# One order table of a fused attention and gated convolution kernel is exchanged for another

## The chip, the core and the metric

The kernel runs on one core of a Trainium2 chip. The metric is the device time in microseconds (us) of one execution; the kernel before took 237.97 us, the median of three runs (237.76 to 238.59). Five engines work side by side, each through its own list of instructions in order: PE (TensorE, matrix products), DVE (VectorE), ACT (ScalarE), POOL (GpSimd) and SP (SyncE, which issues all the DMAs here). An instruction that waits holds up everything behind it on its engine, and nothing on the others until they need it.

## The reference

For 4 batches, 8 heads, 768 positions and a head width of 64, each query sees its neighbours nearer than 16 positions and 24 block summaries (the maximum of the keys and the mean of the values of each block of 32). The 512 wide result then goes through a causal convolution of 5 taps per channel, whose sigmoid gates a linear map, and through a second linear map.

```python
mask_l = np.abs(pos[:, None] - pos[None, :]) < window
scores_s = scale * np.einsum('bhsd,bhnd->bhsn', q, k_sum) + np.log(block)
a = softmax(concatenate([where(mask_l, scores_l, -1e9), scores_s]))
x = a @ concatenate([v, v_sum])             # then heads side by side: B, S, 512
gate = 1 / (1 + exp(-sum_k conv_w[k] * x[s - 4 + k]))
out = (gate * (x @ w_val)) @ w_out
```

## The kernel before

A group g (0 to 11) is 256 positions of one batch; a unit u (0 to 23) is half a group's heads, so that group g holds the units 2g and 2g+1. Most pieces of work come in two halves (.0 and .1) of a unit or of a group.

Nothing in the kernel schedules itself. The string `ORDER` is a list of 955 words; line 729 goes through it, and each word calls one function, which adds its instructions to the lists of its engines. The position of a word against the others of its engine is the order in which that engine works. Tiles come from pools with few buffers (line 54 and the pools of lines 131 to 145); a write into a buffer waits until the earlier tile in it has been read.

```python
for word in ORDER.split():
    nm_ = word.rstrip("0123456789.")
    ops[nm_](*(int(a) for a in word[len(nm_) :].split(".") if a))
```

The words, by engine:

- PE: `W` warm-up products on zeros; `s` scores (L528); `t` transposes of the weights (L579); `x` values (L596, and L598 for group 0); `v` the linear map with w_val (L653, eight passes for group 0, which runs in full float32, twelve for the others); `o` the map with w_out (L690; group 0 has eight small pieces `o0.0.0` to `o0.1.3`, whose last number is the block of 128 columns of w_out); `vb` and `vsp` transposes of block summaries.
- DVE: `n` mask and row extreme (L544); `r` reciprocals of the row sums (L564, L565); `T` the four taps of the convolution (L633); `gf` gate times value (L659); `ks` block maxima of the keys (L225); `sh` and `or`, the two steps that put a block of 64 bit weights together as float32, a shift (L363) and a join (L367); `tv1.3`, one summary of values (L249).
- ACT: `e` exponentials (L557); `c` copies of transposed weights (L586); `X` and `Y` copies of the attention result (L607, L611); `I` the first tap (L627); `G` the gate (L640); `gh` and `ob` copies (L664, L700); `rb` (L358) and `wc` (L403) for the weights.
- POOL: `m` normalising (L569); `Z` and `gl` rests of the split into two parts (L615, L667); `tv` a tree of five additions that sums the values of a block (L253); `kc`, `wl`, `hal` small ones.
- SP: loads `L...` (`Lu` the transposed values for `tv`, `Lv` the values, `Lwo` w_out), `F` which writes block summaries into the value tile (L332), `O` the stores.

A copy `c` frees the one PSUM tile that the transposes `t` of the next half are written to. The value tiles of `Lu` (L209) have two buffers, so a third load waits for a tree on POOL (or, for `tv1.3`, on DVE). The assembled weights `wf` have one buffer of four blocks: w_val's blocks are used up before w_out's are joined into them.

Of the kernel before, what the change touches and what calls it, by code (L numbers as in the profile page):

```python
# [61 lines left out]
vc3.0 vc2.1 vc3.1 vc2.0 s4.1 vb1 n4.0 rbwv2 c1.1 vbc1 n4.1 x1.0 rbwv0 e3.1 rbwv3 wlwv1 m2.1 m2.0
shwv0 shwv2 s5.0 t2.0 x1.1 orwv0 shwv3 orwv2 orwv3 s5.1 Lk1.0 Lk1.1 n5.0 r3 c2.0 Y1 T0.1 n5.1
e4.0 wcwv3 e4.1 v0.1.0 t2.1 v0.0.0 G0 m3.1 wcwv2 Lk1.2 c2.1 wlwv3 m3.0 I1 r4 Lu1.2 v0.1.1 m4.0
F1 Lq3 t3.0 e5.0 m4.1 c3.0 v0.0.1 t3.1 x2.0 e5.1 ks1.1 x2.1 ks1.0 T1.0 c3.1 Lk1.3 wlwv2 X2 Y2
# [2 lines left out]
v1.1.0 n7.1 wlwv0 e6.1 c4.0 rbwo1 v1.1.1 F2 m5.1 m5.0 tv1.1 v1.0.0 t5.0 Lu1.0 Lwo2 v1.0.1 x4.0
e7.0 rbwo0 shwo0 orwo0 shwo1 x4.1 s8.0 orwo1 c5.0 G2 X4 rbwo2 shwo2 s8.1 orwo2 t5.1 Lwo3 Y4 c5.1
wcwo0 gf1.0 r6 rbwo3 e7.1 wcwo2 Lu1.3 o0.0.0 o0.0.1 tv1.3 Lv3 o0.0.2 shwo3 x5.0 orwo3 tv1.0 x5.1  # L70
vsp1 vsc1 m6.0 t6.0 Lq5 o0.0.3 o0.1.0 Lu2.0 Lk3.0 Lu2.2 F3 o0.1.1 o0.1.2 o0.1.3 r7 n8.0 n8.1
s9.0 I3 ob0.0 X5 s9.1 wcwo3 Y5 c6.0 T3.0 T3.1 Z4 m6.1 wlwo0 t6.1 n9.0 e8.0 wcwo1 n9.1 hal2 m7.1
Z5 m7.0 v2.0.0 x6.0 c6.1 G3 I4 gh1.0 x6.1 s10.0 s10.1 gf1.1 t7.1 wlwo2 wlwo1 Lk2.2 Lk2.1 gl1.0
gh1.1 e8.1 X6 T4.0 v2.0.1 v2.1.0 T4.1 ob0.1 O0.0 c7.1 tv2.0 wlwo3 gl1.1 hal3 tv2.2 Y6 G4 t7.0
n10.0 r8 gf2.0 I5 c7.0 e9.0 e9.1 gh2.0 v2.1.1 T5.0 T5.1 Lu2.3 n10.1 o1.0 o1.1 m8.1 t8.1 ob1.0
Lv4 G5 r9 ks2.2 Lk2.0 gf2.1 s11.0 s11.1 I6 T6.0 c8.1 gh2.1 m8.0 gl2.0 e10.0 gl2.1 m9.0 kc2.2
x7.0 x7.1 t8.0 T6.1 n11.0 ks2.1 ks2.0 Lq6 c8.0 ob1.1 X7 Y7 o2.0 Lk2.3 m9.1 Lv5 o2.1 G6 e10.1
ob2.0 F4 I7 Z7 r10 n11.1 Z6 m10.1 kc2.1 kc2.0 T7.0 e11.0 t9.0 v3.1.0 x8.0 x8.1 c9.0 s12.0 T7.1
e11.1 s12.1 t9.1 X8 n12.0 Lu2.1 v3.1.1 n12.1 r11 ks2.3 tv2.3 hal4 m10.0 c9.1 G7 Y8 t10.1 I8
v3.0.0 x9.0 Lq7 O1.0 x9.1 e12.0 c10.1 T8.0 gf3.1 X9 kc2.3 Y9 O1.1 T8.1 s13.0 s13.1 t10.0 c10.0  # L80
e12.1 Z8 m11.0 Z9 ob2.1 F5 tv2.1 v3.0.1 v4.0.0 t11.0 G8 v4.1.0 I9 x10.0 n13.1 n13.0 r12 x10.1
m12.1 s14.0 s14.1 e13.0 c11.0 gf3.0 vsp2 T9.0 T9.1 gh3.0 m11.1 gh3.1 t11.1 X10 vsc2 c11.1 Lk3.3
Y10 Lq8 G9 Lk3.1 v4.1.1 gl3.0 gl3.1 m12.0 I10 n14.1 gf4.1 n14.0 hal5 Z10 o3.0 e13.1 t12.0 c12.0
x11.0 x11.1 s15.0 O2.1 Lv6 s15.1 t12.1 T10.0 v4.0.1 e14.0 e14.1 r13 T10.1 n15.0 m13.1 gf4.0
n15.1 o3.1 Lu3.2 X11 F6 Lv7 G10 O0.1 F7 Y11 Lu3.0 c12.1 r14 I11 m13.0 Z11 m14.1 t13.1 s16.0
T11.0 T11.1 gh4.0 c13.1 ob3.1 ob3.0 e15.0 m14.0 s16.1 x12.0 x12.1 ks3.0 n16.1 t14.1 c14.1 tv3.2
hal6 v5.0.0 t13.0 v5.1.0 v5.1.1 n16.0 ks3.1 Y12 kc3.1 G11 gl4.0 c13.0 X12 I12 x13.0 x13.1 Lq9
s17.0 s17.1 O3.1 Lk3.2 T12.0 gh4.1 e16.0 e15.1 Y13 t14.0 Z12 v5.0.1 T12.1 gf5.1 c14.0 r15 e16.1
ks3.2 kc3.0 n17.0 gf5.0 gl4.1 tv3.0 G12 m15.0 hal7 I13 e17.0 X13 n17.1 o4.1 O3.0 o4.0 s18.0
s18.1 x14.0 x14.1 t15.0 ks3.3 kc3.3 m15.1 Z13 ob4.1 e17.1 X14 v6.1.0 c15.0 T13.0 r16 ob4.0 Y14  # L90
t15.1 T13.1 G13 gh5.0 I14 v6.0.0 v6.1.1 x15.0 O4.1 Lu3.3 O4.0 c15.1 r17 n18.0 n18.1 kc3.2 m16.1
x15.1 gl5.0 T14.0 s19.0 T14.1 e18.0 gh5.1 Y15 e18.1 s19.1 t16.1 v6.0.1 tv3.3 gl5.1 Z14 gf6.1
n19.0 m17.0 m16.0 m17.1 o5.1 gf6.0 o5.0 G14 O2.0 I15 X15 r18 n19.1 c16.1 gh6.1 t16.0 ob5.1 gh6.0
Lv8 Lq10 T15.0 s20.0 Lu3.1 F8 T15.1 s20.1 c16.0 x16.0 m18.0 hal8 Z15 gl6.1 e19.0 x16.1 t18.0 Y16
c18.0 G15 v7.0.0 t17.0 tv3.1 v7.0.1 Lv9 Lq11 I16 c17.0 e19.1 n20.1 t17.1 v7.1.0 gf7.0 n20.0 r19
c17.1 gl6.0 m18.1 m19.1 X16 vsp3 t18.1 x17.0 x17.1 s21.0 c18.1 vsc3 T16.0 s21.1 T16.1 e20.0
t19.1 n21.0 e20.1 v7.1.1 n21.1 gf7.1 r20 m19.0 o6.0 o6.1 s22.0 X17 e21.0 Y17 G16 F9 I17 s22.1
gh7.0 c19.1 gh7.1 ob6.1 T17.0 e21.1 m20.0 T17.1 hal9 Z16 x18.0 x18.1 t19.0 Z17 v8.1.0 O5.1 Lv10
gl7.1 r21 gl7.0 ob5.0 n22.1 o7.0 X18 c19.0 ob6.0 G17 Y18 I18 t20.0 F10 v8.0.0 T18.0 n22.0 x19.0
x19.1 s23.0 c20.0 ob7.0 e22.0 s23.1 m20.1 t20.1 v8.1.1 e22.1 T18.1 Y19 G18 c20.1 I19 X19 m21.0  # L100
O6.0 Lv11 n23.1 n23.0 r22 o7.1 m22.1 Z19 T19.0 gf8.1 t21.0 v8.0.1 c21.0 x20.0 gf8.0 x20.1 O7.0
F11 O6.1 m21.1 Z18 t22.1 v9.1.0 c22.1 gh8.0 Y20 T19.1 gh8.1 G19 I20 X20 m22.0 v9.1.1 t21.1 c21.1
v9.0.0 x21.0 x21.1 hal10 e23.0 t22.0 gl8.0 gf9.1 T20.0 v9.0.1 T20.1 e23.1 r23 Y21 gf9.0 c22.0
G20 X21 ob7.1 gh9.1 gl8.1 I21 T21.0 gh9.0 o8.0 o8.1 m23.1 Z21 hal11 m23.0 gl9.0 ob8.1 gl9.1 o9.1
Z20 t23.1 v10.1.0 x22.0 x22.1 T21.1 O5.0 G21 c23.1 ob9.1 t23.0 X22 I22 Y22 c23.0 v10.0.0 v10.1.1
T22.0 gf10.1 x23.0 x23.1 v10.0.1 gf10.0 T22.1 gh10.1 X23 Y23 ob8.0 gh10.0 O8.1 O7.1 o9.0 ob9.0
gl10.1 Z22 G22 gl10.0 o10.1 Z23 I23 v11.0.0 T23.0 T23.1 v11.0.1 v11.1.0 gf11.0 v11.1.1 ob10.1
gh11.0 O8.0 G23 o10.0 gf11.1 gh11.1 O9.0 O9.1 gl11.0 gl11.1 o11.0.1 o11.1 ob10.0 ob11.0.1 O10.1
ob11.1 O10.0 O11.0.1 O11.1 o11.0.0 ob11.0.0 O11.0.0
# [694 lines left out]
```

## Time and profile before

| what | us |
|---|---|
| median of 3 runs | 237.97 |
| the profiled execution | 237.77 |
| its span, first to last instruction | 236.1 |
| PE busy in it | 224.9 (95%) |
| ACT busy | 190.6 (81%) |
| DVE busy | 184.2 (78%) |
| POOL busy | 152.2 (64%) |

The 1.7 us between the profiled execution's time and its span lie before the first and behind the last instruction. Busy times of the engines overlap; matrix products are pipelined, so the end of a row of PE can lie up to 0.2 us behind the start of the next. In the rows below a bracket at a row's end tells how long the engine was idle before it, and what ended that.

### The profile page before, as it was taken

How to read it: one execution, taken by the hardware profiler on the slowest of the kernel's cores; microseconds unless marked ns; L12 is line 12 of the kernel's file. 1: busy time of each engine (PE TensorE's matmuls, PEld its weight loads, DVE VectorE, ACT ScalarE, POOL GpSimd, SP SyncE). 2: the span in 40 equal slices, each digit the busy share in tenths (PEclk: the TensorE clock that was granted, in tenths of full speed). 3: DMA queues.
4: the chain of work that ended last, by engine and by line, in shares of the span. 5: the costliest groups of instructions: out<-in, count | busy, mean ns of one | idle time of the engine just before them, and what ended most of it. 6: DMA issues, size and time to landing. Idle time of an engine off the chain costs nothing.

```text
span 236.1 us, 7464 instructions
## 1 busy us (share of the span) xinstructions
PE 224.9 (95%) x2734; PEld 196.1 (83%) x2736; DVE 184.2 (78%) x698; ACT 190.6 (81%) x620; POOL 152.2 (64%) x222
## 2 busy tenths in 40 slices
PE   7777999998999999999999999999999999999994
...
GB/s 202 402 408 393 412 280 384 336 115 321 286 170 208 296 254 282 124 310 89 240 98 270 46 186 322 250 40 27 230 77 117 142 95 3 89 3 95 83 56 78
DMA packets 19812, 46.14 MB, mean 195 GB/s; under 512 B 2336, under 2 KB 7200, under 8 KB 19776
## 3 DMA queue, kind: packets, MB, share of 16 engines
...
q8 instruction: 21, 0.34, 0.6%
q14 instruction: 15, 0.12, 0.1%
...
## 4 chain that ended last, share of the span: by engine, by line
PE 78%; DVE 14%; ACT 2%; DMA 2%; issue 1%; SPq 1%; POOL 0%; DVEq 0%; ACTq 0%; POOLq 0%
PE out L690 28%; PE val L653 24%; PE x L596 9%; PE pt L579 8%; PE s L528 8%; DVE g L633 4%; DVE sn L544 3%; DMA q<-in_qT_dram 2%; DVE ks L225 2%; DVE wf L367 2%; DVE wf L363 1%; PE x L598 1%; DVE gf L659 1%; ACT p L557 1%; SPq L204 1%
## 5 line engine op out<-in xcount | busy, mean ns | idle before, releaser
L633 DVE SCALAR_TENSOR_TENSOR g<-xf,cwt,g 128x256 f32<-128x256 f32 x192 | 93.7, 488 | 24.0 <-ACT g L627 12.7
L557 ACT ACTIVATE p<-sn,nm 128x120 f32<-128x120 f32 x192 | 73.3, 388 | 5.8 <-DVE nm L544 5.8
L569 POOL TENSOR_TENSOR p<-p,ri 128x480 f32<-128x480 f32 x48 | 47.3, 998 | 31.2 <-DVE ri L565 19.9
L653 PE MATMUL val<-xh,wv 128*128 128x256 f32 x352 | 50.8, 287 | 0.0
L653 PEld LDWEIGHTS val<-xh,wv 128*128 128x128 f32 x352 | 44.1, 189 | 0.3 <-issue 0.2
L690 PE MATMUL out<-wo,gh 128*128 128x512 f32 (+1 forms) x184 | 44.0, 381 | 0.0
L544 DVE CUSTOM_DVE_ANT_0 sn<-s,mask 128x120 f32<-128x120 f32 x192 | 41.5, 277 | 3.0 <-PE s L528 2.7
L667 POOL TENSOR_TENSOR gl<-gf,gh 128x512 fp32r<-128x512 f32 x22 | 28.1, 1287 | 21.8 <-ACT gh L664 21.7
L690 PEld LDWEIGHTS out<-wo,gh 128*128 128x128 f32 x184 | 32.8, 188 | 5.9
L586 ACT COPY pts<-pt 120x512 f32<-120x512 f32 x48 | 28.0, 584 | 11.6 <-PE pt L579 11.5
L557 ACT ACTIVATION_READ_ACCUMULATOR p<-sn,nm 128x1 f32 x192 | 37.1, 193 | 0.0
L579 PE MATMUL pt<-ident,p 128*120 128x128 f32 x192 | 30.0, 279 | 2.9 <-ACT pts L586 2.1
L615 POOL TENSOR_TENSOR xl<-xf,xh 128x512 fp32r<-128x512 f32 x22 | 28.4, 1296 | 3.9 <-ACT xf L611 3.2
L596 PE MATMUL x<-pts,v 120*64 120x64 f32 x768 | 30.2, 225 | 0.0
L596 PEld LDWEIGHTS x<-pts,v 120*64 120x64 f32 x768 | 26.2, 137 | 3.9 <-issue 1.5
L528 PE MATMUL s<-k,q 64*64 64x120 f32 x768 | 25.9, 269 | 2.1 <-POOL k L239 0.6
L579 PEld LDWEIGHTS pt<-ident,p 128*120 128x120 f32 x192 | 21.2, 137 | 7.8 <-POOL vpad L287 1.7
L253 POOL TENSOR_TENSOR vT<-vT 128x384 f32<-128x384 f32 (+3 forms) x44 | 25.9, 589 | 2.6
L653 PE MATMUL val<-xl,wv 128*128 128x256 f32 x176 | 27.5, 278 | 0.0
L528 PEld LDWEIGHTS s<-k,q 64*64 64x64 f32 x768 | 19.9, 132 | 7.2 <-issue 2.4
L659 DVE SCALAR_TENSOR_TENSOR gf<-gt,val 128x512 f32<-128x512 f32 x24 | 16.3, 679 | 10.5 <-PE val L653 10.1
L690 PE MATMUL out<-wo,gl 128*128 128x512 f32 (+1 forms) x92 | 23.8, 380 | 0.0
...
## 6 DMA issues: line engine op xcount, KB each, us to landing
...
```

The source lines that it names most:

```text
L528: nc.tensor.matmul(sp(u)[64 * e : 64 * e + 64, h, c * KW : c * KW + KW], qt(g)[64 * h : 64 * h + 64, pr, i * QT : i * QT + QT], ktile[b, p ...
L544: nc.vector.tensor_tensor_reduce(sn(u)[:, n, :], sp(u)[:, h, c * KW : c * KW + KW], mask[:, mv, :], -1.0 / math.sqrt(D), 3.0e38, ALU.add, ...
L557: nc.scalar.activation(pr_(u)[:, n, :], sn(u)[:, n, :], AF.Exp, bias=nm(u)[:, n : n + 1], scale=-1.0, accum_out=rs(u)[:, n, 0:1],)
L569: nc.gpsimd.tensor_tensor(pr_(u)[:, w], pr_(u)[:, w], st["ri", u][:, w].unsqueeze(2).broadcast_to([P, TPU, KW]), ALU.mult,)
L579: nc.tensor.transpose(pt[:KW, i, :], pr_(u)[:, TPU * r + i, :], ident)
L586: nc.scalar.copy(dst, src)
L596: nc.tensor.matmul(dst, v[:KW, i, c0 : c0 + D], src, start=True, stop=g > 0)
L615: nc.gpsimd.tensor_tensor(xl(g)[:, two(hp), :], xf(g)[:, two(hp), HALO:], xh(g)[:, two(hp), :].bitcast(F32), ALU.subtract,)
L633: nc.vector.scalar_tensor_tensor(gp(u)[:, r], xf(g)[:, pr, o : o + SG], cwt[:, pr, o : o + 1], gp(u)[:, r], ALU.mult, ALU.add,)
L653: nc.tensor.matmul(pp[:, r], w, x, start=(n == 0), stop=(n == len(terms) - 1))
L667: nc.gpsimd.tensor_tensor(gl(g)[:, two(cp), :], grp["gf", g, cp], gh(g)[:, two(cp), :].bitcast(F32), ALU.subtract)
L690: nc.tensor.matmul(pp, x, w, start=(n == 0), stop=(n == len(terms) - 1))
```

## The change

The string `ORDER` is replaced. The 955 words are the same, each once, so every instruction, buffer, load and home stays; only their order differs. On the whole the pieces of work come in the same sequence, and neighbours have changed places. Two lines of the old and two of the new table:

```diff
@@ ORDER @@
-Lk0.0 wz Lk0.1 Mu ez cv W0 Lp0 W1 Lc W2 W3 W4 Lk0.2 W5 Lp1 W6 W7 W8 Mm Lp2 ks0.0 Lk0.3 ks0.1 Lp3
...
-kc1.1 kc1.0 T1.1 ks1.2 t4.1 Lv2 Lu1.1 Lwo1 ks1.3 s6.0 Lq4 s6.1 hal1 tv1.2 x3.0 Lwo0 x3.1 G1 I2
...
+Lk0.0 ez wz W0 Lk0.1 W1 Mu Mm W2 Lp0 W3 W4 W5 W6 Lc ks0.0 Lk0.2 ks0.1 kc0.0 Mi cv kc0.1 W7 W8 W9
...
+wlwv2 hal1 c3.1 x2.1 ks1.3 ks1.2 s6.0 t4.1 X2 Y2 s6.1 c4.1 G1 kc1.3 Lwo3 Lwo0 x3.0 x3.1 kc1.2
...
```

ACT, from the copy of unit 3's second half (`c3.1`) on: `pts` is the copied tile, `xh` and `xf` are the words `X` and `Y`, L640 is `G` and L627 is `I`. Before:

```order
L586 COPY pts_3_664<-pt_3_1_670 120x512
L607 CAST xh_1_708<-x_2_675 128x512
L611 COPY xf_1_710<-x_2_675 128x2x256
L640 ACTIVATE gt_0_625<-g_1_634 128x512
L627 ACTIVATE g_2_782<-xf_1_710,cwt_104 128x256 x2
L586 COPY pts_4_785<-pt_4_1_722 120x512
L607 CAST xh_1_708<-x_3_762 128x512
L611 COPY xf_1_710<-x_3_762 128x2x256
L403 CAST wv_109<-wf_111 128x512
```

ACT after, from the same copy:

```order
L586 COPY pts_3_679<-pt_3_1_688 120x512
L607 CAST xh_1_737<-x_2_694 128x512
L611 COPY xf_1_708<-x_2_694 128x2x256
L586 COPY pts_4_748<-pt_4_1_732 120x512
L640 ACTIVATE gt_0_568<-g_1_597 128x512
L627 ACTIVATE g_2_797<-xf_1_708,cwt_104 128x256 x2
L611 COPY xf_1_708<-x_3_757 128x2x256
L607 CAST xh_1_737<-x_3_757 128x512
L586 COPY pts_4_748<-pt_4_0_780 120x512
```

The copy `c4.1` (pts_4 from pt_4_1) has moved from behind `G1` and `I2` to ahead of them; `X3` and `Y3` have changed places, and `c4.0` follows them at once.

DVE, the joins of w_out, from the first shift on (the row that ends each block's preparation is L367, its source `sc_wo` with the block's number). Before:

```order
L363 TENSOR_SCALAR wf_111<-raw_wo0_771 128x512
L367 SCALAR_TENSOR_TENSOR wf_111<-sc_wo0_952,wf_111 128x512
L363 TENSOR_SCALAR wf_111<-raw_wo1_732 128x512
L367 SCALAR_TENSOR_TENSOR wf_111<-sc_wo1_878,wf_111 128x512
L363 TENSOR_SCALAR wf_111<-raw_wo2_924 128x512
L367 SCALAR_TENSOR_TENSOR wf_111<-sc_wo2_981,wf_111 128x512
L659 SCALAR_TENSOR_TENSOR gf_1_0_1004<-gt_1_977,val_1_0_904 128x512
L564 TENSOR_REDUCE ri_6_1006<-rs2_114 128x8
L565 RECIPROCAL ri_6_1006<-ri_6_1006 128x8
L249 TENSOR_REDUCE vsT_1_3_1027<-vT_1_3_1016 128x24
L363 TENSOR_SCALAR wf_111<-raw_wo3_998 128x512
L367 SCALAR_TENSOR_TENSOR wf_111<-sc_wo3_1009,wf_111 128x512
```

DVE after:

```order
L363 TENSOR_SCALAR wf_111<-raw_wo0_755 128x512
L363 TENSOR_SCALAR wf_111<-raw_wo1_778 128x512
L367 SCALAR_TENSOR_TENSOR wf_111<-sc_wo0_898,wf_111 128x512
L659 SCALAR_TENSOR_TENSOR gf_0_1_917<-gt_0_568,val_0_1_644 128x512
L659 SCALAR_TENSOR_TENSOR gf_1_0_961<-gt_1_910,val_1_0_848 128x512
L367 SCALAR_TENSOR_TENSOR wf_111<-sc_wo1_912,wf_111 128x512
L564 TENSOR_REDUCE ri_6_964<-rs2_114 128x8
L565 RECIPROCAL ri_6_964<-ri_6_964 128x8
L363 TENSOR_SCALAR wf_111<-raw_wo2_967 128x512
L363 TENSOR_SCALAR wf_111<-raw_wo3_753 128x512
L367 SCALAR_TENSOR_TENSOR wf_111<-sc_wo2_979,wf_111 128x512
L367 SCALAR_TENSOR_TENSOR wf_111<-sc_wo3_827,wf_111 128x512
```

The summary `tv1.3` (L249) no longer stands ahead of block 3; `gf0.1` has come in from a place far ahead; the shifts and joins of two blocks stand together.

SP, from the loads of batch 1's values to the load of group 3's values (`v_3`). Before:

```order
L209 DMA vT_1_1_730<-in_vT_dram 128x768
L382 DMA raw_wo1_732<-in_wo_dram 128x4x256
L200 DMA q_4_745<-in_qT_dram 128x1024
L382 DMA raw_wo0_771<-in_wo_dram 128x4x256
L332 DMA v_2_727<-vb_108 12x2x512 x4
L209 DMA vT_1_0_922<-in_vT_dram 128x768
L382 DMA raw_wo2_924<-in_wo_dram 128x4x256
L382 DMA raw_wo3_998<-in_wo_dram 128x4x256
L209 DMA vT_1_3_1016<-in_vT_dram 128x768
L216 DMA v_3_1029<-in_vw_dram 128x1024 x2
```

SP after:

```order
L382 DMA raw_wo3_753<-in_wo_dram 128x4x256
L382 DMA raw_wo0_755<-in_wo_dram 128x4x256
L209 DMA vT_1_0_776<-in_vT_dram 128x768
L382 DMA raw_wo1_778<-in_wo_dram 128x4x256
L332 DMA v_2_685<-vb_108 12x2x512 x4
L200 DMA q_4_892<-in_qT_dram 128x1024
L209 DMA vT_1_1_950<-in_vT_dram 128x768
L382 DMA raw_wo2_967<-in_wo_dram 128x4x256
L209 DMA vT_1_2_1026<-in_vT_dram 128x768
L209 DMA vT_1_3_1034<-in_vT_dram 128x768
L216 DMA v_3_1107<-in_vw_dram 128x1024 x2
```

The load of batch 1's third summary (`vT_1_2`), which stood ahead of these rows, now stands third of four; `vT_1_3` is last in both, and `v_3` follows it. On POOL `tv1.2` stands ahead of `Z2` before, and `tv1.1` and `tv1.0` behind `m5.0`; after, `tv1.0`, `tv1.1` and `tv1.2` stand in a row behind `m5.1`.

On PE the pieces of group 0's output stand before as `o0.0.0 o0.0.1 o0.0.2 x5.0 x5.1 vsp1 t6.0 o0.0.3 o0.1.0`, after as `o0.0.0 o0.1.0 o0.1.1 o0.0.1 o0.0.2 o0.0.3 x5.0 x5.1`. Ahead of the first `v`, PE had `s5.0 t2.0 x1.1 s5.1 v0.1.0 t2.1` and has `t2.0 x1.1 s5.0 s5.1 t2.1 v0.0.0`; on DVE `T0.1` has moved from behind `n5.0` to ahead of the joins of w_val. Later on PE `s6.0` has moved from behind `t4.1` to ahead of it. The last four words of PE (`o10.0 o11.0.1 o11.1 o11.0.0`) are the same.

## Rows read from the trace of the kernel before

**Rows 1.** The page: busy time of each engine, and PE in 40 equal slices of the span, in tenths.

```profile
PE 224.9 (95%) x2734; PEld 196.1 (83%) x2736; DVE 184.2 (78%) x698; ACT 190.6 (81%) x620; POOL 152.2 (64%) x222
...
PE   7777999998999999999999999999999999999994
```

**Rows 2.** Busy time of each engine in stretches of the span: stretch, length, then PE, PEld, DVE, ACT, POOL busy with their instructions, granted TensorE clock, DMA share, GB/s.

```profile
6.00:12.00 6.00, 4.28 (x65) 2.03 (x67) 5.17 (x31) 4.10 (x21) 1.76 (x8) 1.00 1.03 403
...
24.00:30.00 6.00, 5.49 (x116) 4.28 (x106) 4.81 (x24) 5.27 (x16) 1.43 (x2) 1.00 1.02 412
...
66.00:228.00 162.00, 162.00 (x1890) 145.64 (x1889) 124.43 (x451) 133.83 (x424) 107.22 (x139) 1.00 0.46 149
```

**Rows 3.** PE in order of time: start, length, what. The second half of unit 5's scores and the first `v`, the waits between 39 and 44 us, and the pieces of group 0's output.

```profile
29.27 0.64 PE L528 MATMUL s<-k,q 64*64 64x120 f32 x16
29.85 1.99 PE L653 MATMUL val<-xf,wf 128*128 128x256 f32 x8
...
39.94 0.62 PE L579 MATMUL pt<-ident,p 128*120 128x128 f32 x4 [0.35 <-ACT pts L586]
40.49 1.05 PE L528 MATMUL s<-k,q 64*64 64x120 f32 x32
...
42.84 0.65 PE L579 MATMUL pt<-ident,p 128*120 128x128 f32 x4 [0.21 <-ACT pts L586]
43.59 1.05 PE L528 MATMUL s<-k,q 64*64 64x120 f32 x32
...
53.24 2.84 PE L690 MATMUL out<-wf,gf 128*128 128x128 f32 x24
56.01 1.15 PE L596 MATMUL x<-pts,v 120*64 120x64 f32 x32
...
58.94 4.73 PE L690 MATMUL out<-wf,gf 128*128 128x128 f32 x40 [0.80 <-DVE wf L367]
63.60 1.05 PE L528 MATMUL s<-k,q 64*64 64x120 f32 x32
```

**Rows 4.** ACT in order of time, from `G1` to `X3`.

```profile
40.65 0.60 ACT L640 ACTIVATE gt<-g 128x512 f32<-128x512 f32 x1
41.28 0.99 ACT L627 ACTIVATE g<-xf,cwt 128x256 f32<-128x256 f32 x2
42.21 0.58 ACT L586 COPY pts<-pt 120x512 f32<-120x512 f32 x1
42.69 0.58 ACT L607 CAST xh<-x 128x512 fp32r<-128x512 f32 x1
```

**Rows 5.** DVE in order of time: its one long wait between 20 and 60 us, and the joins of w_out.

```profile
29.98 0.28 DVE L544 CUSTOM_DVE_ANT_0 sn<-s,mask 128x120 f32<-128x120 f32 x1 [1.07 <-PE s L528]
...
50.29 0.42 DVE L363 TENSOR_SCALAR wf<-raw_wo 128x512 uint32<-128x512 uint32 x1
...
54.77 0.68 DVE L659 SCALAR_TENSOR_TENSOR gf<-gt,val 128x512 f32<-128x512 f32 x1
...
55.67 0.90 DVE L249 TENSOR_REDUCE vsT<-vT 128x24 f32<-128x768 f32 x1
56.49 0.70 DVE L363 TENSOR_SCALAR wf<-raw_wo 128x512 uint32<-128x512 uint32 x1
57.30 1.58 DVE L367 SCALAR_TENSOR_TENSOR wf<-sc_wo,wf 128x512 uint32<-128x512 uint32 x1
58.80 0.16 DVE L564 TENSOR_REDUCE ri<-rs 128x8 f32<-128x16 f32 x1
```

**Rows 6.** Groups of instructions by line and shape: xcount, busy us, mean ns of one, idle before.

```profile
L253 POOL TENSOR_TENSOR vT<-vT 128x384 f32<-128x384 f32 x11 | 11.3, 1028 | 0.0
...
L367 DVE SCALAR_TENSOR_TENSOR wf<-sc_wo,wf 128x512 uint32<-128x512 uint32 x4 | 4.4, 1088 | 0.3
...
L367 DVE SCALAR_TENSOR_TENSOR wf<-sc_wv,wf 128x512 uint32<-128x512 uint32 x4 | 2.7, 686 | 0.0
```

**Rows 7.** POOL in order of time: the normalising of unit 5 and the trees `tv1.1` and `tv1.0` (four of the five additions of each).

```profile
46.32 1.93 POOL L569 TENSOR_TENSOR p<-p,ri 128x480 f32<-128x480 f32 x2
48.21 2.62 POOL L253 TENSOR_TENSOR vT<-vT 128x384 f32<-128x384 f32 x4
...
51.56 3.41 POOL L253 TENSOR_TENSOR vT<-vT 128x384 f32<-128x384 f32 x4
```

**Rows 8.** SP in order of time: the load of `vT_1_3` and the loads behind it, and, later, the load `Lv6` with the fill `F6` that waits for its landing.

```profile
51.63 0.34 SPq L209 DMA_DIRECT2D vT<-in_vT_dram  x1
52.06 0.86 SPq L216 DMA_DIRECT2D v<-in_vw_dram  x2
...
101.36 0.93 SPq L216 DMA_DIRECT2D v<-in_vw_dram  x2
...
109.14 3.30 SPq L332 DMA_DIRECT2D v<-vs  x4
```

**Rows 9.** A `Z` on POOL and the `v` on PE that reads it; a copy on ACT and the `x` on PE that reads it.

```profile
97.95 1.29 POOL L615 TENSOR_TENSOR xl<-xf,xh 128x512 fp32r<-128x512 f32 x1 [0.47 <-ACT xf L611]
...
99.57 1.10 PE L653 MATMUL val<-xh,wv 128*128 128x256 f32 x8
...
151.69 0.58 ACT L586 COPY pts<-pt 120x512 f32<-120x512 f32 x1 [2.05 <-PE pt L579]
...
152.56 0.63 PE L596 MATMUL x<-pts,v 120*64 120x64 f32 x14
```

More of the change, by code (lines that the diff above doesn't have):

```diff
@@ L62 @@
[L62 to L65, printed above, removed]
-kc1.1 kc1.0 T1.1 ks1.2 t4.1 Lv2 Lu1.1 Lwo1 ks1.3 s6.0 Lq4 s6.1 hal1 tv1.2 x3.0 Lwo0 x3.1 G1 I2
-c4.1 Z2 n6.1 n6.0 t4.0 gf0.1 r5 kc1.2 kc1.3 T2.0 X3 Y3 wcwv0 e6.0 s7.0 s7.1 n7.0 gf0.0 T2.1 Z3
@@ L68 @@
[L68 to L109, printed above, removed]
+Lk0.0 ez wz W0 Lk0.1 W1 Mu Mm W2 Lp0 W3 W4 W5 W6 Lc ks0.0 Lk0.2 ks0.1 kc0.0 Mi cv kc0.1 W7 W8 W9
```

57 lines of the change are left out of this document (52 added, 5 removed).

## The prediction, as it went on record

> **What bounds the kernel now.** I read the page first. PE is busy 224.9 of 236.1 us, and its slices show where the rest lies: in the first eight and in the last [rows 1]. The table of stretches says the same in numbers: 1.72 us of six are idle from 6 to 12, 0.51 from 24 to 30, and from 66 to 228 us PE is busy 162.00 of 162 [rows 2]. So no order can gain anything behind 66 us; an order can only lose there. What can be won lies ahead of it: the time at which PE arrives at 66 us with the same work done. For that I read PE in order of time and looked for brackets [rows 3]. Behind 30 us there are four gaps: 0.35 at 39.94, 0.21 at 42.84, 0.10 at 43.59 (the row before ends at 42.84 + 0.65 = 43.49) and 0.80 at 58.94; the first two name ACT's copy, the last DVE's join of a weight block. The granted TensorE clock is 1.00 in all these stretches [rows 2], so only order is at stake.
>
> **The change, part by part.** Instructions, shapes and loads are the same, so their busy time is taken as unchanged, and each part is a gap that closes or opens.
>
> *A, scores of unit 5.* Before, its two halves stand apart, and one alone takes 0.64; two together take 1.05 [rows 3]. After they stand together: 2 x 0.64 - 1.05 = 0.23. I take 0.2. The ends are 0 and 0.23; a loss is excluded, since the pair does the same passes in one row.
>
> *B, the gaps at 39.94, 42.84 and 43.59, together 0.66.* The first: `t4.1` waits for the copy `c3.1`. After, `s6.0` stands ahead of it, half of a 1.05 row, so 0.5 of work lies over 0.35 of waiting. The second: `t4.0` waits for `c4.1`, which ends at 42.21 + 0.58 = 42.79 and stands behind `G1` (from 40.65) and `I2` (from 41.28) [rows 4]. Without these two it begins 42.21 - 40.65 = 1.56 earlier. What pays for it is `X3`, now behind `Y3`: one copy, 42.69 - 42.21 = 0.48, so it begins at about 43.2 on the clock of before, and its reader, the first `v` of group 1, comes about 1 us later (two halves of scores, 1.05, from 43.59). That is covered. The third gap follows the second, but a DVE piece may be behind it. I take 0.6. The ends are 0.66 and -0.5, one copy's place, if `X3` is late after all.
>
> *C, the gap of 0.80 at 58.94.* Five pieces of group 0's output take 63.60 - 58.94 = 4.66, 0.93 each [rows 3]. Before, the join of block 3 was wanted by the fourth piece; after by the sixth, which begins at 53.24 - 0.8 (A and B) + 5 x 0.93 = 57.1. On DVE the shifts and joins ran from 50.29 to 57.30 + 1.58 = 58.88, 8.59 us, with `tv1.3` (0.82, from 55.67 to 56.49) among them [rows 5]. After, `tv1.3` is out and `gf0.1` (0.68) is in: 8.45. They begin earlier by that 0.68, since `gf0.1` stood ahead before, and by 1.07, the wait at 29.98 for scores, which now has `T0.1` ahead of it: 48.54. The end is 56.99, and the sixth piece at 57.1 finds its block with 0.1 to spare. If the 1.07 isn't won, the end is 58.06, the wait 0.95, and the part costs 0.15. Ends: -0.15 and 0.8. I take 0.7, near the upper one, since the rows of DVE show the wait and name what it waited for.
>
> *D, from 66 us on.* PE has no idle time there, but little cover: a `Z` that ends at 97.95 + 1.29 = 99.24 is read at 99.57, and a copy that ends at 151.69 + 0.58 = 152.27 is read at 152.56 [rows 9]. Cover of 0.3 against one copy's place, 0.48, opens a gap of 0.2. One such gap is my value; none, or seven (1.4), are the ends, since the trace doesn't show the new order. The last four pieces of PE are the same, so the tail costs nothing.
>
> Sum: 0.2 + 0.6 + 0.7 - 0.2 = 1.3. The profiled execution took 237.77, so 236.47; the median of before lies 0.20 above it, so 236.7.
>
> **A rule that speaks against C.** The joins of w_val took 686 ns, those of w_out 1088 in the mean and 1.58 us at most [rows 5, 6]; the latter lay beside POOL's trees [rows 7]. The Trainium skill (SBUF — State Buffer, "SBUF: two separate sides") states that a DVE operation with two inputs in SBUF and a GpSimd operation that reads SBUF take a shared port for a whole instruction each, while the other stands still. The trace agrees as far as the longer joins go. By that rule alone each of the four joins could wait for one whole first addition of a tree (1028 ns): 4.1 us, where before lost 1.6; C would be 0.8 - 2.4 = -1.6, and the time 239.0. The sum above doesn't use it: it keeps the loss of before.
>
> **Rivals.**
>
> *1. The joins collide more, and C is eaten up.* After, three trees follow `m5.1` where before there were two, from 48.21 to 51.56 + 3.41 = 54.97 [rows 7], so all four joins lie beside one. For it: the rows 6. Against it: two of the four of before collided already. If each loses as much as the worst (1.58 - 0.69 = 0.89), the loss is 3.6 in place of 1.6, the joins end at 59.0, PE waits 1.9, C is -1.1 and the time 238.5; half of it gives 237.5. I put this rival at 238.0.
>
> *2. DVE waits for the load of `tv1.3` (the slower side).* That load takes the buffer of a tree. Before, it was issued at 51.63, right behind the first tree of two, and `tv1.3` began at 55.67 without an idle time: it landed within 4.04 us [rows 5, 8]. After, it needs the second tree of three, 54.97 on the clock of before and 54.2 with A and B. Landed within 4.04 it is there at 58.2; DVE comes to it at 56.99 and the two halves of `n8` later (eight such rows as that at 29.98, 0.2 each by their starts): 58.6. That is 0.4 of cover. If it takes as long as the load issued until 101.36 + 0.93 = 102.29, whose fill could begin at 109.14, 6.85 us [rows 8], it is there at 61.05, DVE waits 2.45, and comes to `T3.0` at 62.3, 1.5 behind before (58.80 + 0.4 + 1.6 = 60.8). With 0.3 of cover on PE [rows 9], PE is 1.2 behind, and A, B and C are lost: 237.97 + 1.2 = 239.2. It decides from a landing at about 60 us on. Against it: at 51.63 the load had two others right behind it, as it will have. I put it at 239.0.
>
> *3. The head wins more.* Ahead of 30 us PE idles too [rows 2]. After, `t1.0` stands ahead of unit 3's scores and its copy ahead of `Y0`, so a wait of `t1.1` there may shrink; by steps from the rows of ACT I find that the next thing, a copy of block summaries, is ready at the same time as before, so I count nothing. If half of the 1.72 + 0.51 closes, 1.1 more: 235.6.
>
> **How the numbers follow.** My forecast has 0.50, its own range 235.9 to 237.3 (C lost or D empty, not both at once). Rival 1 has 0.20, rival 2 0.18, rival 3 0.12. A difference of under 0.3%, 0.7 us, can't be told from none, so faster is under 237.26 and slower over 238.68. Faster: 0.46 of the forecast, 0.02 of rival 1, 0.12 of rival 3, 0.60. Same: 0.04, 0.15 and 0.03 of rival 2, 0.22. Slower: 0.03 of rival 1 and 0.15 of rival 2, 0.18. The range for 8 in 10 goes from 235.3 to 238.9: rival 3 with some room, rival 1 whole, and rival 2 up to its point.
>
> **What would show it.** In PE's rows after: the two scores of unit 5 as one row of 1.05 (A); no bracket at `t4.1` and `t4.0`, and the first `v` of group 1 at about 43.8 in place of 44.57 (B); the six pieces of group 0's output without a bracket, and DVE's last join ending at about 57 (C); PE busy 161.8 or more of the 162 us that end where its first rest used to be (D). Rival 1 shows as joins of over 1.1 us in the mean and a bracket naming L367; rival 2 as a bracket at L249 on DVE that names a DMA or at `T3.0` behind 60.8; rival 3 as PE busy over 5.5 us of 6 already ahead of 24 us. The prediction is wrong if PE idles behind 66 us for over 1 us in all, since no part of it has a gap there.

## The result, and the profile after

The kernel after took 239.91 us (median of 20 executions, 238.56 to 242.02), the kernel before beside it 238.10 (20 executions, 237.46 to 239.94). The ratio is 1.0085, 95% interval 1.0064 to 1.0105: slower by 0.85%. The forecast was 236.7, faster, with 235.3 to 238.9 as its range; it was wrong in sign and outside the range. The profiled execution took 238.6, near the lowest, so its trace shows less than half of what the median lost. Six of the twenty show a mean granted clock of 0.992 or 0.993 and took 240.7 to 242.0, the other fourteen 238.6 to 241.0; the second trace below shows one execution of the former kind.

The table of stretches of the kernel after, columns as in [rows 2]:

```profile
66.00:72.00 6.00, 4.56 (x85) 4.03 (x84) 5.72 (x27) 5.58 (x22) 6.00 (x7) 1.00 1.02 339
72.00:228.00 156.00, 155.59 (x1789) 139.59 (x1787) 117.86 (x418) 125.94 (x397) 102.59 (x135) 1.00 0.45 145
```

Where PE had no idle time behind 66 us [rows 2], it now has 1.44 us within six (66 to 72) and 0.41 in the rest, 1.85 in all: that is over the 1 us which the prediction named as the sign that it is wrong. In order of time PE shows the place:

```profile
28.41 1.23 PE L528 MATMUL s<-k,q 64*64 64x120 f32 x32
...
39.58 0.65 PE L579 MATMUL pt<-ident,p 128*120 128x128 f32 x4
...
41.82 0.65 PE L579 MATMUL pt<-ident,p 128*120 128x128 f32 x4
42.84 1.05 PE L528 MATMUL s<-k,q 64*64 64x120 f32 x32 [0.37 <-DMA v<-vb]
...
52.47 5.52 PE L690 MATMUL out<-wf,gf 128*128 128x128 f32 x48
...
67.89 1.05 PE L528 MATMUL s<-k,q 64*64 64x120 f32 x32
70.05 0.34 PE L596 MATMUL x<-pts,v 120*64 120x64 f32 x4 [1.10 <-DMA v<-vs]
70.72 1.03 PE L596 MATMUL x<-pts,v 120*64 120x64 f32 x28 [0.34 <-DMA v<-vs]
...
118.78 1.32 PE L596 MATMUL x<-pts,v 120*64 120x64 f32 x32 [0.25 <-DMA k<-in_kT_dram]
```

The head is mostly as forecast: no bracket at `t4.1` and `t4.0`, the first `v` of group 1 at 43.82 (43.8 was forecast), and the six pieces of group 0's output in one row without a wait, where before 0.80 us stood [rows 3]. Only the row of unit 5's scores (28.41) takes 1.23 and not 1.05. At 70.05 `x6.0` waits for `v<-vs`: the fill `F3` (L332), four DMAs of 48 KB that write the block summaries of batch 1 into the values of group 3.

To add this up I use a *lead*: the time at which PE, in the trace of before, had done the same sum of matrix work (each form at its own duration), less the time at which it has in this trace; all are set to nothing at `s1.1` (12 us), since the landing of the first queries moves by a microsecond and more from one execution to the next. The names of the runs are those of the next section.

| trace | `x5.0` (58 us) | `s10.1` (68) | `o1.0` (74) | `x12.1` (119) | end |
|---|---|---|---|---|---|
| after | 1.6 | 1.9 | 0.0 | -0.4 | -0.5 |
| after, second trace | 1.5 | 1.8 | -2.2 | -2.5 | -2.5 |
| pe_fill | 1.3 | 1.5 | 0.6 | 0.2 | -0.3 |
| f3_first | 1.4 | 1.7 | 1.6 | 1.4 | 1.3 |
| lv_first | 1.5 | 1.8 | 1.6 | 1.2 | 1.1 |
| lv3_only | 1.0 | 1.1 | 1.1 | 0.1 | -1.3 |
| f6_early | 1.4 | 1.7 | 0.0 | 0.1 | 0.2 |
| spfix | 1.8 | 2.0 | 1.9 | 2.0 | 2.1 |

(spfix reached `s1.1` 2.2 later than the kernel before. Part of such a delay is made up by 30 us, so its entries are a little high; what counts is how they go on. lv3_only's trace is that of its slowest execution, with a granted clock of 0.95 in every stretch behind 6 us where the others show 1.00.) So by 58 us the traces of the new order's head have won 1.3 us or more, lv3_only's 1.0, and the first trace of the kernel after loses all of it at one instruction.

Why the fill is late stands in SP's rows, from the loads of transposed values (L209) on:

```profile
44.30 0.43 SPq L382 DMA_DIRECT2D raw_wo<-in_wo_dram  x1
51.20 4.08 SPq L209 DMA_DIRECT2D vT<-in_vT_dram  x2
55.37 0.86 SPq L216 DMA_DIRECT2D v<-in_vw_dram  x2
56.33 0.38 SPq L200 DMA_DIRECT2D q<-in_qT_dram  x1
56.76 0.45 SPq L204 DMA_DIRECT2D k<-in_kT_dram  x1
58.15 0.33 SPq L209 DMA_DIRECT2D vT<-in_vT_dram  x1
58.53 1.06 SPq L204 DMA_DIRECT2D k<-in_kT_dram  x1
59.64 0.52 SPq L706 DMA_DIRECT2D out_dram<-ob  x1
60.20 0.57 SPq L204 DMA_DIRECT2D k<-in_kT_dram  x1
62.23 3.49 SPq L332 DMA_DIRECT2D v<-vs  x4
```

and in the end of the chain of waits that leads to `x6.0` (start, length, what):

```profile
64.94 5.64 DMA v<-vs
...
70.72 1.03 PE x L596 x28
```

From 44.73 SP issues nothing for 6.5 us, then one load, then nothing until the second tree has ended: `Lu1.2` and `Lu1.3` each wait for a tree on POOL. Behind them stands `Lv3` (two DMAs of 512 KB, 55.37), which before went out at 52.06, behind one such load [rows 8]. Then everything goes out at once: with `Lq5` 3.6 MB from 55.37 to 60.77, which at the 350 GB/s of this stretch is over 10 us of transfer. Into this come the four small DMAs of the fill, and the last of them lands 5.64 us after its issue.

### The profile page after: what moved, and what is told of

Same layout as the page of the kernel before. It is cut to its first block, busy times and chain, and to the rows that moved or that the text cites. A ratio compares the mean times of both kernels' runs of the same rounds, so it can differ in the third digit from the quotient of the medians.

```text
span 236.9 us, 7481 instructions
## 1 busy us (share of the span) xinstructions
PE 223.9 (95%) x2736; PEld 196.1 (83%) x2736; DVE 182.8 (77%) x698; ACT 191.4 (81%) x620; POOL 152.2 (64%) x222
## 4 chain that ended last, share of the span: by engine, by line
PE 70%; DMA 11%; ACT 6%; POOL 5%; SPq 3%; issue 2%; DVE 1%; ACTq 0%
PE val L653 24%; PE out L690 21%; PE x L596 9%; PE pt L579 8%; PE s L528 7%; DMA k<-in_kT_dram 5%; DMA q<-in_qT_dram 4%; DMA v<-vs 2%; POOL vT L253 2%; ACT p L557 2%; SPq L332 1%; POOL p L569 1%; ACT pts L586 1%; PE warm_out L298 1%; DVE sn L544 1%
## 5 line engine op out<-in xcount | busy, mean ns | idle before, releaser
L569 POOL TENSOR_TENSOR p<-p,ri 128x480 f32<-128x480 f32 x48 | 46.8, 986 | 15.7 <-DVE nm L544 7.6
L586 ACT COPY pts<-pt 120x512 f32<-120x512 f32 x48 | 28.0, 583 | 8.8 <-PE pt L579 8.1
L653 PEld LDWEIGHTS val<-xl,wv 128*128 128x128 f32 x176 | 23.5, 189 | 0.0
```

The source lines that it names most:

```text
L569: nc.gpsimd.tensor_tensor(pr_(u)[:, w], pr_(u)[:, w], st["ri", u][:, w].unsqueeze(2).broadcast_to([P, TPU, KW]), ALU.mult,)
L586: nc.scalar.copy(dst, src)
L653: nc.tensor.matmul(pp[:, r], w, x, start=(n == 0), stop=(n == len(terms) - 1))
```

## The experiments

Each kernel is the kernel after with words of `ORDER` moved, unless it says otherwise. In the first four the table is wrapped wider, so their line numbers are ten lower (L586 is `x`, L322 the fill).

**pe_fill: something else for PE to do**

```diff
-s10.1 ... x6.0 x6.1 t7.0 ... v2.1.1 gf2.0 o1.0
+s10.1 ... v2.1.1 x6.0 x6.1 t7.0 ... gf2.0 o1.0
```

> The kernel after, with one word moved: the product `v2.1.1` (1.5 us on PE) stands ahead of `x6.0`. Theory 1 (the lead of 2.0 us that PE has at 68.4 is lost in one wait, at `x6.0`, for the fill `F3` of block summaries, because `vsp1` now stands only 8.5 us ahead of its reader): the wait of 1.1 + 0.34 shrinks to under 0.3, PE is 1.5 us or more ahead of the kernel before at `o1.0`, and the time falls by 1.3 or more from the 239.9 of the kernel after, to 238.6 or less. Rival 2 (DVE's wait for the load of `tv1.3`, or the trees, set the time behind 60 us): another piece waits in place of `x6.0` and the time stays at 239.5 to 240.3. Rival 3 (the time above the profiled 238.6 comes from drops of the clock that have nothing to do with this wait): the profiled time falls by 1.5, but the executions still spread over 3 us.

Measured: 238.56 (12 executions), ratio 1.0020 (0.9998 to 1.0041) to before. PE in order of time:

```profile
71.25 0.34 PE L586 MATMUL x<-pts,v 120*64 120x64 f32 x4
71.83 1.03 PE L586 MATMUL x<-pts,v 120*64 120x64 f32 x28 [0.24 <-DMA v<-vs]
```

The time falls by 1.3, as expected, but the lead at `o1.0` is 0.6 and not 1.5: the fill is still in the way by a few tenths, and `x6` took 1.6 from start to end in place of 1.15. 0.5 more goes at `s22.0` (171 us), which waits for a load of queries. So the wait at `x6.0` is a large part of the loss, and filling it from PE's side doesn't cure it.

**f3_first: the fill ahead of the five issues in front of it**

```diff
-Lk2.1 Lu2.1 ... Lk3.0 ... O0.0 Lk2.2 F3
+F3 Lk2.1 Lu2.1 Lk3.0 O0.0 Lk2.2
```

> The kernel after, with the five issues that stand ahead of the fill `F3` on SP (`Lk2.1`, `Lu2.1`, `Lk3.0`, `O0.0`, `Lk2.2`, about 2 MB) put right behind it. Theory 1a (the fill lands late because these loads fill the DMA engines when it is issued): it is issued from 62.2 as now, lands by 67.5 in place of 70.6, and `x6.0` doesn't wait: time 238.6 or less, the same as with `v2.1.1` ahead. Rival 1b (the fill takes its 8.3 us from `vsp1` whatever stands ahead of it): the wait at `x6.0` keeps 1.0 us or more, and the time stays above 239.4.

Measured: 237.22 (12 executions, 236.41 to 243.08), ratio 0.9965 (0.9947 to 0.9983): faster than before. SP's row of the fill, and PE's of its reader:

```profile
62.59 3.30 SPq L322 DMA_DIRECT2D v<-vs  x4
```

```profile
69.24 1.15 PE L586 MATMUL x<-pts,v 120*64 120x64 f32 x32
```

The fill is issued no earlier than in the kernel after (62.59 against 62.23), and yet `x6.0` doesn't wait. It is the 2 MB in front that made it land late; 1b has fallen. PE keeps 1.3 us to the end.

**f6_early: the later fill alone**

```diff
-gf4.1 Lv7 I11 o3.0 e15.0 F6 Lk3.1
+gf4.1 F6 Lv7 I11 o3.0 e15.0 Lk3.1
-gh3.1 Y10 m13.1 m13.0 X10 G9 ... e14.0 vsc2
+gh3.1 vsc2 Y10 m13.1 m13.0 X10 G9 ... e14.0
```

> The kernel after, with the copy `vsc2` on ACT back ahead of `Y10` and the fill `F6` on SP back ahead of the load `Lv7`, as both stood before. The wait of 0.25 at `x12.0` and its slow weight loads (1.32 in place of 0.69) go: 0.5 us less behind 119 us, and nothing else changes; the wait at `x6.0` stays. Time 239.4 (0.5 under the kernel after). If the loss behind 100 us is spread over other places, it stays at 239.9.

Measured: 240.97 (7 executions, 238.97 to 242.92), ratio 1.0106 (1.0068 to 1.0145), no gain. SP's rows, and PE's at `x12.0`:

```profile
105.49 1.01 SPq L206 DMA_DIRECT2D v<-in_vw_dram  x2
112.34 3.30 SPq L322 DMA_DIRECT2D v<-vs  x4
```

```profile
119.59 1.15 PE L586 MATMUL x<-pts,v 120*64 120x64 f32 x32
```

In the trace the edit does what was expected of it: `x12.0` has no wait, and from `o1.0` to the end PE loses nothing (0.0 to 0.2 in the table), where the first trace of the kernel after loses 0.5. The fill goes out at 112.34 against 112.50, but this execution reached `s1.1` 1.1 later, so counted from there it goes out 1.3 earlier. It could have gone at 109, when its copy is done; from then on it waits for the landing of `Lv6`, issued at 105.49 behind `Lu3.0`, which waits for a tree. The wait at `x6.0` is still there (0.89 and 0.36). Why the median is no lower this trace, an execution of 239.24, doesn't show.

**all3: these three edits together**

> The kernel after with all three edits. If the two waits for fills are all that the new order loses in its middle, the lead of 2.0 us holds to 130 us, and 0.4 to 0.8 is lost behind it (as in the kernel after: 0.35 by 170 us and 0.4 in the tail): 236.6 to 237.2, faster than the kernel before by 0.3 to 0.6%. If something else takes the lead, 238 or more.

Measured: 237.39 (12 executions, 236.75 to 243.46), ratio 0.9970 (0.9946 to 0.9994): between the two values expected, and no more than `F3` alone. The profiled execution was the one of 243.46, so it says nothing about the median; its chain of waits shows how one slow landing is handed on (start, length, what):

```profile
106.07 7.83 DMA v<-in_vw_dram
...
117.87 7.13 DMA v<-in_vw_dram
...
130.15 6.37 DMA k<-in_kT_dram
...
142.40 0.62 PE pt L569 x4
```

A load of `vT` lands at 101, the tree runs, `Lu3.0` goes out, behind it `Lv6`; its landing releases `F6`, behind it `Lv7`, whose landing releases `F7`, behind it the keys, and their maxima on DVE hold up a unit's exponentials on ACT until PE has waited 2.0 us, from 140.4 to 142.4. `F6` and `F7` were issued at 113.97 and 125.06, where the first trace of after has 112.50 and 118.00. SP is a chain here: each wait for a landing holds the next load.

**lv_first: the loads of values ahead of the waiting loads**

```diff
-Lwo2 Lu1.2 Lu1.3 Lv3 Lq5        (and)  Lu3.0 O0.1 Lk3.2 Lv6
+Lwo2 Lv3 Lu1.2 Lu1.3 Lq5        (and)  Lv6 Lu3.0 O0.1 Lk3.2
```

> The kernel after with two words moved: the loads `Lv3` and `Lv6` ahead of the loads `Lu1.2` and `Lu3.0` that wait for trees. `F3` stays behind the five loads. If the five loads are what makes the fill late (1a), `x6.0` still waits 0.6 to 1.1, since only the 1.37 us in which `F3` waits for `Lv3` go and `vsc1` ends at 61.7 anyway; `x12.0` doesn't wait: time 239.0 to 239.6. If it is the wait for `Lv3` alone (1c), `x6.0` is free and the time is that of `F3` ahead, 237.2.

Measured: 237.59 (12 executions, 236.77 to 238.82), ratio 0.9978 (0.9960 to 0.9996). SP, and PE at `x6.0`:

```profile
45.99 0.81 SPq L216 DMA_DIRECT2D v<-in_vw_dram  x2
...
62.12 3.31 SPq L332 DMA_DIRECT2D v<-vs  x4
```

```profile
69.27 1.15 PE L596 MATMUL x<-pts,v 120*64 120x64 f32 x32
```

My value, 239.0 to 239.6, was wrong, and so were both its reasons. The fill still goes out at 62.12 behind the same five issues, and `x6.0` doesn't wait: 1 MB has left the burst and is issued at 46 us. It is moved by about 52: from 50 to 52 the DMA engines, at a share of 0.01 in the kernel after, are now at 0.63. What counts is neither the wait for `Lv3` nor those five loads as such, but the sum of bytes in front of the fill.

**lv3_only: one word**

```diff
-Lwo2 Lu1.2 Lu1.3 Lv3 Lq5
+Lwo2 Lv3 Lu1.2 Lu1.3 Lq5
```

> The kernel after with one word moved: the load `Lv3` (1 MB) ahead of the load `Lu1.2`, so it is issued at about 46 us, into idle DMA engines, in place of 55.4. Theory, as the run with both `Lv` words moved has left it (the fill is late by the bytes that were issued between 55 and 62 us, after SP had stood behind two trees; 1 MB less of them is 2.9 us at 350 GB/s, more than the wait): `x6.0` doesn't wait, PE keeps 1.3 us or more at 72 us, the wait at `x12.0` stays, and the time is 237.6 to 238.1. If it took both words, the wait at `x6.0` is back at over 0.5 and the time over 238.8.

Measured: 237.73 (12 executions, 236.88 to 239.86), ratio 0.9979 (0.9958 to 0.9999), within what was expected. One word out of 955 takes the kernel from 0.85% slower to 0.2% faster. PE at `x6.0`:

```profile
70.06 1.15 PE L596 MATMUL x<-pts,v 120*64 120x64 f32 x32
```

`x6.0` doesn't wait, and the wait at `x12.0` stays (0.43), both as expected. The lead at `o1.0` is 1.1 and not 1.3, and none is left at the end; but this is the execution of 239.86 with the clock of 0.95, so it doesn't show what an execution near the median keeps.

**before_late_f3: the reverse, on the kernel before**

```diff
-Lu2.2 F3 ... Lk2.2 Lk2.1 O0.0 ... Lk2.3
+Lu2.2 Lk2.2 Lk2.1 Lk2.3 F3 ... O0.0
```

> The kernel before with one thing of the kernel after: three loads of keys (`Lk2.2`, `Lk2.1`, `Lk2.3`, 0.49 MB each) stand ahead of the fill `F3` on SP. PE's order and all else is that of before. Theory 1a: at 350 GB/s they delay the fill by up to 4.2 us; its last part was issued at 62.5 and `x6.0` ran at 66.54 without waiting, so `x6.0` waits 0.5 to 4 us with a bracket naming the fill, and the time is 0.5 to 4 above that of before: 239.5 as my value. Rival (PE's order, not the loads, makes the wait): no wait at `x6.0`, 237.9 to 238.2.

Measured: 240.88 (6 executions, 239.45 to 244.67), ratio 1.0100 (1.0062 to 1.0138). SP, and PE in order of time:

```profile
56.96 1.43 SPq L204 DMA_DIRECT2D k<-in_kT_dram  x3
59.42 4.60 SPq L332 DMA_DIRECT2D v<-vs  x4
```

```profile
68.64 1.44 PE L596 MATMUL x<-pts,v 120*64 120x64 f32 x32 [2.00 <-DMA v<-vs]
```

With PE's order untouched, 1.4 MB in front of the fill give the kernel before a wait at the same place, and a loss as large as that of the whole change.

**after_again: the kernel after, unchanged**

> The kernel after once more, unchanged, for a second trace. Theory: the head is again ahead by 1.5 us or more at 68 us (apart from what the first load of q takes), and what is lost is lost in waits for `F3`, `F6` or another fill, of 1.1 us or more each where the time is above 239.5. Rival: the time is 239.5 or more with waits no longer than in the first trace.

Measured: 240.87. The last piece of the chain of waits ahead of `x6` (start, length, what), and the stretches behind it, columns as in [rows 2]:

```profile
65.17 6.38 DMA v<-vs
```

```profile
72.00:74.00 2.00, 2.00 (x32) 1.93 (x28) 1.93 (x4) 0.87 (x2) 2.00 (x3) 0.69 1.02 417
74.00:76.00 2.00, 2.00 (x11) 2.00 (x11) 1.86 (x5) 2.00 (x9) 1.36 (x2) 0.50 1.02 418
76.00:78.00 2.00, 2.00 (x11) 1.66 (x10) 1.45 (x3) 2.00 (x10) 1.26 (x2) 0.95 0.36 144
```

Here the fill's last part landed 6.38 after its issue, PE waited 1.76 and 0.27, and about a microsecond after the second wait the granted clock fell to 0.50, which is 1.2 in place of 2.4 GHz, until about 76 us. The loss between `s10.1` and `o1.0` is 3.9; 2.3 of it is there when the `x` are done, and 1.6 is the slow clock behind them. The mean clock of this execution is 0.993, which is that of the six of the twenty named above. It fits them, but a mean doesn't show the place: spfix's trace has 0.993 too, and its clock was at 0.50 from 10 to 12 us, in the head.

**b_only: part B by itself, on the kernel before**

```diff
-t4.1 ... ks1.3 s6.0 ... x3.1 G1 I2 c4.1
+s6.0 t4.1 ... ks1.3 ... x3.1 c4.1 G1 I2
```

> The kernel before with part B alone: `s6.0` ahead of `t4.1` on PE and the copy `c4.1` ahead of `G1` and `I2` on ACT. Theory (a gap closed ahead of a wait that stays where it is, is handed on to that wait): the gaps at `t4.1` and `t4.0` close, but DVE's joins don't move, so the wait at the piece `o0.0.3` grows from 0.80 to 1.1 or more, and the time is that of before, 237.9 to 238.3: B is worth its 0.6 only together with C. The sum as the forecast made it (each part alone): 237.5, with the wait at `o0.0.3` unchanged.

Measured: 238.13 (12 executions), ratio 0.9997 (0.9985 to 1.0010). PE:

```profile
43.89 1.05 PE L528 MATMUL s<-k,q 64*64 64x120 f32 x32 [0.61 <-POOL k L239]
...
59.31 4.73 PE L690 MATMUL out<-wf,gf 128*128 128x128 f32 x40 [0.82 <-DVE wf L367]
```

Both gaps close and nothing is won, as expected, but not by the way expected: the wait at `o0.0.3` is the same, and `s7.0`, three rows on, now waits 0.61 for POOL's copy of key maxima (0.10 before). In the kernel after those copies stand earlier on POOL, which the forecast hadn't priced.

**tail_only and combo: the two orders welded at 73 and 83 us**

```diff
-(tail_only, words 1 to 371) the order of after
+(tail_only, words 1 to 371) the order of before, to v2.1.1
-(combo, behind t8.0) the order of after
+(combo, behind t8.0) the order of before; ahead of it Lv3 and F3 as in spfix
```

> The first 371 words in the order of before (to `v2.1.1`, 73 us on PE), the rest in that of the kernel after. It measures step D apart from the head and from `x6.0`. From the first trace of the kernel after, which loses 1.0 us from 72 us to the end (0.5 at `x12.0`, 0.35 by 170 us in steps of about 0.1, the rest in the tail): 238.1 + 1.0 = 239.1. The forecast's D would give 238.3. Rival (the rest loses only because a head that is ahead leaves its loads less time): 238.1.

> The other way round: the head of the kernel after with SP's queue mended (`Lv3` ahead of `Lu1.2`, `F3` ahead of its loads) up to `t8.0` (83 us on PE), and behind it the order of before, with the trees of block 2 put where their loads allow. If head and rest add up, PE keeps its 1.4 us to the end: 236.4 to 236.9. If the loads of the rest have no cover for a PE that comes 1.4 earlier, waits for fills or keys take 0.5 or more of it, and the time is 237.2 or above.

Measured: 240.76 and 243.16 (6 executions each), ratios 1.0095 (1.0069 to 1.0121) and 1.0194 (1.0171 to 1.0218), far from any value expected. Both measure their seam, combo mostly and tail_only for 0.87 of the 1.8 that it loses behind 73 us, as PE's row of tail_only shows:

```profile
86.84 0.73 PE L690 MATMUL out<-wo,gl 128*128 128x512 f32 x2 [0.87 <-POOL gl L667]
```

In combo PE waits 1.78 ahead of 89.92 and 2.48, for POOL's copy of keys, ahead of 93.98. One thing can be read from tail_only: from 100 to 160 us PE has no idle time, and 0.47 from 160 to 228, at `s22.0`, which waits for `Lq11`. So D by itself was not measured, and whether head and rest add up these two don't tell.

**spfix: SP's queue put right**

```diff
-Lwo2 Lu1.2 Lu1.3 Lv3 Lq5 Lk2.1 Lu2.1 Lk3.0 O0.0 Lk2.2 F3
+Lwo2 Lv3 Lu1.2 Lu1.3 Lq5 F3 Lk2.1 Lu2.1 Lk3.0 O0.0 Lk2.2
-Lu3.0 O0.1 Lk3.2 Lv6 Lv7 F6     (and on ACT)  Y10 X10 ... vsc2
+Lv6 Lu3.0 O0.1 Lk3.2 F6 Lv7     (and on ACT)  vsc2 Y10 X10
-Lv10 F9 O5.0 Lq11
+Lq11 Lv10 F9 O5.0
```

> The kernel after with SP's queue put so that no load of values (`Lv`) stands behind a load of transposed values (`Lu`) that waits for a tree: `Lv3` ahead of `Lu1.2`, `Lv6` ahead of `Lu3.0`; `F3` ahead of its five loads and `F6` ahead of `Lv7`, `vsc2` ahead of `Y10`, `Lq11` ahead of `Lv10`. Theory (what the new order loses is lost in SP's queue: a landing is waited for by a fill, behind which the next load stands, so that a slow transfer is handed on): `x6.0` and `x12.0` don't wait, `F3` and `F6` are issued as soon as `vsc1` and `vsc2` have ended (61.7 and 106.5), and executions above 239 don't occur: median 236.3 to 236.9, highest under 239. Rival (slow transfers cost the same whatever the order on SP): median as with `F3` alone ahead, 237.2, and one execution in ten above 240.

Measured: 237.15 (12 executions, 236.27 to 238.30), ratio 0.9953 (0.9928 to 0.9978): it beats both kernels, and its highest execution lies below the lowest of the kernel after. The median is 0.25 above my range. PE in the stretch of [rows 2], and SP's row of `F6`:

```profile
66.00:228.00 162.00, 162.00 (x1891) 145.73 (x1891) 125.65 (x457) 133.55 (x423) 110.80 (x142) 1.00 0.49 161
```

```profile
108.37 3.36 SPq L332 DMA_DIRECT2D v<-vs  x4
```

PE is full from 66 to 228 us, as it was before. `F6` goes out 4 us earlier than in f6_early. Whether it is better than f3_first (0.9965) these intervals don't tell.

## Why the prediction was wrong

*A and B* (0.2 and 0.6): at group 0's first two `v` the lead of the first trace is 0.1 and 0.2, as forecast, though the pair of unit 5's scores takes 1.23 and by itself gives only 0.05. The lead at the first `v` of group 1 is 0.6 in the first trace (0.5 in lv_first), against 0.8, so B is 0.4. The two gaps closed, and `s7.0` waits 0.37 where 0.10 stood. The pieces were right, but b_only shows that B doesn't stand alone: a gap is worth its length only if the next operand is early too, and here a third engine, POOL, had to move for it.

*C* (0.7): 1.0, from `v1.1.0` to `x5.0`, above its upper end of 0.8. On DVE, in order of time, and the group of the joins by line (columns as in [rows 6]):

```profile
52.21 0.68 DVE L367 SCALAR_TENSOR_TENSOR wf<-sc_wo,wf 128x512 uint32<-128x512 uint32 x1
...
54.09 1.38 DVE L367 SCALAR_TENSOR_TENSOR wf<-sc_wo,wf 128x512 uint32<-128x512 uint32 x2
...
57.97 0.95 DVE L249 TENSOR_REDUCE vsT<-vT 128x24 f32<-128x768 f32 x1 [0.87 <-DMA vT<-in_vT_dram]
...
59.15 0.96 DVE L633 SCALAR_TENSOR_TENSOR g<-xf,cwt,g 128x256 f32<-128x256 f32 x2
```

```profile
L367 DVE SCALAR_TENSOR_TENSOR wf<-sc_wo,wf 128x512 uint32<-128x512 uint32 x4 | 2.8, 723 | 0.0
```

The last join ends at 55.47, 1.5 ahead of the 56.99 worked out, since the joins took 723 ns and not the 1088 kept from [rows 6]. With that rival 1 has fallen. A, B and C together were forecast at 1.5 and are 1.3 to 1.8 at `x5.0`, lv3_only's 1.0 apart: this half of the sum was right, in part by luck, since B came out lower and C higher.

POOL's trees ran beside all four joins, as rival 1 had it, but it was POOL that lost the time. In order of the chain of waits (start, length, what), the second addition of the first tree, with no join beside it, and that of the second tree:

```profile
49.00 0.60 POOL vT L253
...
52.23 1.14 POOL vT L253
```

The join at 52.21 had begun just ahead of that addition and took its usual 0.68. The same holds for the last join (54.76) and the third tree's first addition (54.89), which took 1.45 where that of the other two trees took 1.0. Before, it was the other way round: the join of 1.38 began at 51.91 inside an addition that had begun at 51.56, and the one of 1.58, at 57.30 [rows 5], inside this `Z` (POOL in order of time):

```profile
56.87 1.46 POOL L615 TENSOR_TENSOR xl<-xf,xh 128x512 fp32r<-128x512 f32 x1
```

So the prediction read [rows 7] wrongly here: the trees of before had ended at 55.3, and its longest join met no tree. The rule of the Trainium skill that was set against C (SBUF — State Buffer, "SBUF: two separate sides": a whole instruction each, the other standing still) fits these rows of both kernels: what had begun first ran on, and the other took longer. The order of the words doesn't tell which begins first, and at 52.2 it was a matter of 0.02 us, so the size of C was in part luck, though all ten traces of the new head show it.

*D* (0.2 lost from 66 us on) is the step that failed. It priced one open gap of 0.2 from the cover between engines, a `Z` and a copy [rows 9], and the prediction said that no part of it had a gap behind 66 us. From `s10.1` to the end the first trace loses 2.4 and the second 4.3. The gaps that D had in mind stayed shut: with SP's queue put right PE is busy 162.00 of 162. What opened was cover of another kind, which the forecast never read: from the issue of a DMA to the reader of what it writes. In the first trace `F3` costs 1.9 (1.9 to 0.0 in the table), `x12.0` 0.4, and the rest 0.1 to 0.2; in the second, `F3` and the clock behind it 3.9. lv3_only and f3_first show that the first is caused by the bytes issued ahead of the fill: either edit takes it away, and the reverse edit puts it into the kernel before.

*Rival 2* had the mechanism and looked at the wrong reader. It said that a load behind a third tree would be late, followed it to `tv1.3` on DVE, and found cover; it did come late there (0.87 of waiting at 57.97), and DVE was at `T3.0` by 59.15, ahead of the 60.8 from which it would have cost anything. What stood behind that load on SP, `Lv3`, and the fill behind `Lv3`, it didn't follow. The rows for it were there: [rows 8] has the load `Lv6` issued until 102.29 and its fill at 109.14, 6.85 us. The same behind `Lv3`, which in the first trace is issued until 56.23, puts `F3` at 63.1 and the end of its four issues (3.30 in the same rows) at 66.4, which leaves its last part 2.5 us to land before PE comes to `x6.0` at 68.9.

The Trainium skill (DMA: Bandwidth & Descriptors, "Queues, rings and completion order") states that the copies one sequencer issues run on one row of rings, and that the descriptors of a ring are taken in order. The traces agree: the last part of the fill, issued at 64.94 and 65.17, landed after 5.64 and 6.38 us behind the whole burst, and in lv_first, issued at 64.65, within the 4.62 until `x6.0` ran unhindered.

*Rival 3* (more from the head): not seen; the lead at the first `v` (30.05) is under 0.2, which is part A.

What stays open: why spfix wins 0.95 to 1.1 in the median where its trace shows more, and how an execution near the median of the kernel after spends its time, since the two traces are of 238.6 and 240.87 and no trace lies between. That one word takes the median from slower to faster shows that most of the loss hangs on `F3`, but not how it is shared between the wait and the clock.
